# Half of each key and value load added onto the other half by the DMA

## The chip, the cores and the metric

One Trainium2 core runs the kernel. It has TensorE (PE; PEld is its weight load), VectorE (DVE), ScalarE (ACT), GpSimd (POOL) and SyncE (SP), each with its own instruction queue that is worked off in order, and 16 DMA engines that all queues share. The metric is the device time of one execution in microseconds (us). A profiled execution comes beside the timed ones; times "from the span's start" are read from its trace.

## The reference

Attention with pooled keys and values, then a feed-forward layer with a maximum of three products. All inputs and the output are f32.

```python
# q, k, v: (8, 8, 576, 64) = batch, heads, rows, head width
k_p = k.reshape(B, H, 72, 8, D).mean(axis=3)        # mean of each eight rows
v_p = v.reshape(B, H, 72, 8, D).mean(axis=3)
scores = scale * np.matmul(q, k_p.transpose(0, 1, 3, 2))
attn = softmax(scores)
attn_out = np.matmul(attn, v_p)
x = attn_out.transpose(0, 2, 1, 3).reshape(B * S, H * D)      # 4608 x 512
h = np.maximum(np.maximum(x @ w1, x @ w2), x @ w3)            # 512 -> 768
out = h @ w_out                                                # 768 -> 512
```

The change touches the two means: eight rows of keys, or of values, are added up for each of 8 x 72 groups in each of the 8 batches. (The kernel forms sums; the factor 1/8 is put in elsewhere.)

## The kernel before

**Stages.** Attention runs by batch (576 rows each), the feed-forward by block of 512 rows (9 blocks). The work of a batch is laid between the products of the block before, so that TensorE always has something: block n carries the attention of batch n + 1. The order is written out by hand. `block(0, ...)` is the first stage; the dictionary `MIDDLE` holds one string for each of the blocks 1 to 5, which `middle(n)` plays; `ORDER` holds the rest. In `MIDDLE` a step `h` is a product of the feed-forward (`-` begins it, `+` puts its end), a digit is an output product, `a`, `b`, `f` and `S` are VectorE sums, `k` turns folded keys for the scores, `s` are scores, `v` the product with the values, `x` the transpose of its result, `T` the transposed load of queries. A stage between 53 and 160 us takes some 21.5 us.

**Loads.** From batch 1 on, `load_k`, `load_v` and `load_q` (L73 to L101) each bring 576 KB (written) of one batch from memory by a GpSimd DMA, which reads f32 and writes f16 or bf16: 1.18 MB are read. Each kind of tile has two buffers, so batch b + 2 goes where batch b was. A step such as `k5<` in `MIDDLE` issues the load of keys of batch 5.

**Folds.** `fold_steps` (L157) adds the eight rows in three adds: four rows to four rows into `half` (L163, in two parts in the middle stages), two to two (L165), one to one into `kp` (keys) or `vp` (values) (L167). GpSimd does it from batch 2 on for keys and for values of batch 1 and later. `k5+2` plays two of the four instructions of the keys of batch 5.

**What ties GpSimd.** `pool_step` (L879) plays these steps. A load is tied to the last feed-forward product so far, `mms[-1]`, and to the last transposed load of queries, `turned`:

```python
op = load()
for x in (mms[-1], *turned):
    after([op], x)
return
```

After a `!` the next fold instruction is tied to the last VectorE sum (`held[:] = gate`). GpSimd waits for what an instruction needs and all behind it in its queue waits too.

**What uses the folds.** `keys` (L200) transposes `kp` on TensorE (the pkt matmuls of L202), `turn_k` copies the result to `kz` (L213), the scores use that (L226). `values` (L298) multiplies with `vp` (L302). The queries come through `load_q`, and from batch 3 on through a DMA transpose from SyncE's queue (L349), which waits for the queries' landing.

Of the kernel before, what the change touches and what calls it, by code (L numbers as in the profile page):

```python
# [10 lines left out]
ALU = mybir.AluOpType  # L11
# [3 lines left out]
def kernel(  # L15
# [11 lines left out]
    nc = tc.nc  # L27
# [39 lines left out]
    def after(loads, first):  # L67
        for x in loads:
            tc.add_manual_dep(x.ins, first.ins.name, mybir.DependencyInfo(
                mybir.DependencyClass.Sync, mybir.DependencyReason.DATA),  # L70
                reason="weights first")

# [81 lines left out]
    def fold(e, t, out, dtype=F32):  # L154
        return list(fold_steps(e, t, out, dtype))

# [713 lines left out]
    load_k(3, nc.gpsimd)  # L870
    load_v(3, nc.gpsimd)
    load_q(3)
    fold_k(2, nc.gpsimd)
    fold_v(2)
# [4 lines left out]
    def pool_step(n, name):  # L879

        what, b = name[0], int(name[1])
        if name[2:] == "<":
            load = {"k": lambda: load_k(b, nc.gpsimd), "v": lambda: load_v(b, nc.gpsimd),
                    "q": lambda: load_q(b)}[what]
            op = load()
            for x in (mms[-1], *turned):
                after([op], x)
            return
        if (what, b) not in folding:
            if what == "k":  # L890
                new_kp(b)
                folding[what, b] = fold_steps(nc.gpsimd, kts[b], kps[b], parts=2)
            else:
                folding[what, b] = fold_steps(nc.gpsimd, vts[b], vp_all[:, b, :, 0:D],
                                                  parts=2)
        for _ in range(int(name[3:])):
            op = next(folding[what, b])
            for x in held:
                after([op], x)
            held.clear()  # L900
# [14 lines left out]
    def weave():  # L915

        products, seen, outs = {}, {}, out_seven(5)
        for name in ORDER.split():
            if name == "F":
                next(tiles)  # L920
            elif name == "vpool":
                held[:] = gate
                pool_step(5, "v7+4")
# [25 lines left out]
    MIDDLE = {  # L949
        1: """  # L950
            h- q4< k4< h+ 1:x2 1:v4- h- h- v4< h+ 1:v4+ h+ h- 1:x3 h- h+ h+ h- 1:x4 h+ h- k-
            h- h+ h+ q0 h h- k+ h+ h q1 h s0- s0+ s0+ q2 h- s0+ h- s0+ h+ b1 S q3 h+ h- S S
            3:T S h+ a3 s3- a1 s3+ s3+ h- s3+ h- h+ h+ a2 h- s3+ a4 s6- s6+ 1- s6+ h+ b3 b2
            b4 v0 2- 1+ 6- x0 v1 7- v2- 6+ x1 5- 2+ 7+ v2+ ! k3+4 v3- v3+2 v3+ 5+ v4 3- x2
            4- x3 3+ 4+ x4
        """,
        2: """
            h k5< k- h- k+ h+ a1 a3 h- a2 f a4 f ! v3+2 v5< h+ f s0- s0+ s0+ s0+ h- h- h- h+
            h+ s0+ h- h+ s3- h+ h- f s3+ h- s3+ h+ h- s3+ b1 s3+ s6- h+ s6+ h- h+ h- s6+ !
            k4+2 h+ h+ b2 b3 b4 ! k4+2 1- 4:T v0- 1+ v1- v0+ x0 2- v1+ 6- v2- 7- x1 2+ 7+  # L960
            v4+2 6+ v2+ 5- v3- 5+ v3+ x2 x3 v4 x4 3- 4 3+
        """,
        3: """
            k- q5< k+ a3 k6< h a1 h- h- h+ a2 s0- f a4 ! v4+2 s0+ s0+ f h- h+ s0+ h+ s0+ h-
            h- h+ h+ s3- h- v6< h+ h s3+ s3+ s3+ s3+ h- b1 h- h+ h+ s6- s6+ ! k5+2 h h- s6+
            1- h+ b2 b3 b4 1+ ! k5+2 v5+2 v0- 2- v0+ x0 v1 6- 2+ x1 6+ 7- 5:T 7+ v2- 5- v2+
            x2 v3- 5+ v3+ v4 x3 3 x4 4
        """,
        4: """
            h- q6< h+ k- h- k+ a1 a2 f h+ h- a3 a4 ! v5+2 h- f h+ k7< h+ s0- s0+ h- h- s0+  # L970
            s0+ h+ s0+ h+ 6:T h- s3- h+ s3+ s3+ s3+ h- s3+ h+ h- b1 h+ h ! k6+2 s6- s6+ h h
            b3 b2 b4 s6+ ! k6+2 1- v6+2 v0 2- 1+ x0 v1- 6- v1+ 2+ x1 v2 7- 6+ 5- x2 v3 6:k-
            x3 7+ 5+ 3- 6:k+ v4 x4 4- 3+ 4+
        """,
        5: """
            h q7< a1 v7< h- a2 h- a3 h+ h+ a4 ! v6+2 h- s0- s0+ h+ s0+ h- s0+ s0+ h- h- k7+4
            h+ h+ s3- h+ 7:T s3+ h- s3+ h- s3+ s3+ h+ s6- h+ s6+ s6+ h h- v0 h+ h- x0 v1- h+
            v1+ x1
        """}
    folds = iter([f for wi in range(1, 3) for f in [fold_w(wi)] * 4])  # L980

    def middle(n):

        pieces, outs, out_tiles = hidden(n), None, project(n)
        for name in MIDDLE[n].split():
            if name[0] == "h":
                parts(name, lambda: next(pieces))
            elif name == "F":
                next(out_tiles)
            elif name == "f":  # L990
                next(next(folds))
            elif name == "!":
                held[:] = gate
            elif name[0].isdigit() and name[1:] in ("", "+", "-"):
                outs = outs or out_seven(n)
                parts(f"o{name}", lambda: outs(int(name[0]), 0, 1))
            elif name[0] in "ab":
                sums_of(n, name)
            elif name[2:3] == "<" or name[2:3] == "+" and name[3:]:
                pool_step(n, name)  # L1000
            else:
                b, _, step = name.rpartition(":")
                do(int(b or n + 1), step)
        assert next(pieces, None) is None

    tt_all.append(const.tile([128, 4, 5, HALF], F16, name="tt", tag="tt"))
    for n in range(1, 6):
        middle(n)
# [50 lines left out]
```

## Time and profile before

| what | value |
|---|---|
| median of the runs | 227.42 us (227.27 to 227.57, 2 runs) |
| profiled execution: time / span | 227.08 / 225.4 us |
| granted TensorE clock | 1.00 |
| busy: TensorE / VectorE / ScalarE / GpSimd | 212.3 / 161.4 / 120.3 / 140.9 us |
| DMA queue of GpSimd (q0) | 16944 packets, 16.98 MB, 47.8% of 16 engines |
| DMA queue of SyncE (q1) | 29888 packets, 15.87 MB, 31.1% |
| GpSimd's first adds (L163) of values / keys in halves | 10 of 2.12 us / 10 of 1.64 us |
| second adds (L165) of values / keys | 7 of 2.47 us / 6 of 1.81 us |
| last adds (L167) of values / keys | 7 of 1.36 us / 6 of 0.99 us |

Busy times are instruction times put end to end without double counting; an engine that is not the bottleneck loses nothing by idling. A wait is idle time on an engine, with the engine or the DMA that ended it. A DMA's landing is counted from the start of its issue. A DMA share of 1 means that packets were under way on all 16 engines; as several queues can be under way at once it can be above 1 in a short stretch.

### The profile page before, as it was taken

What the parts mean: (1) busy time and instruction counts of PE and PEld (TensorE: products, weight loads), DVE (VectorE), ACT (ScalarE), POOL (GpSimd) and SP (SyncE); (2) the same over time, 40 slices, a digit from 0 to 9 for tenths busy, and PEclk for the clock granted to TensorE, in tenths of its full rate; (3) what the DMA queues carried; (4) which work ended last, traced back from release to release, by engine and by line L of the source; (5) the groups of instructions that cost most, each with busy time, mean ns of one, the idle gap of its engine ahead of it and who ended that gap; (6) DMA issues with size and microseconds to landing.
All of it is one profiled execution on the core that took longest, in us unless ns stands there. A gap on an engine that the chain in (4) does not pass through costs nothing.

```text
span 225.4 us, 4876 instructions
## 1 busy us (share of the span) xinstructions
PE 212.3 (94%) x1884; PEld 147.1 (65%) x1885; DVE 161.4 (72%) x314; ACT 120.3 (53%) x233; POOL 140.9 (63%) x121
## 2 busy tenths in 40 slices
PE   6688999999999999999999999999799999999993
PEld 2477744458658645964685468547589667788882
DVE  3668898036997796776679668729767977878940
ACT  2267524855883576237724842693694445564330
POOL 7974300999939969775885769794292903881020
PEclk9999999999999999999999999999999999999999
DMA  6999999999649999649967999699530755200265
GB/s 179 209 197 197 211 203 209 202 168 230 115 105 156 168 176 247 122 61 214 252 85 154 221 202 151 86 236 166 109 56 19 163 102 113 47 0 3 66 198 159
DMA packets 47303, 33.55 MB, mean 149 GB/s; under 512 B 26992, under 2 KB 42288, under 8 KB 47280
## 3 DMA queue, kind: packets, MB, share of 16 engines
q0 software_dynamic: 16944, 16.98, 47.8%
q1 hardware_dynamic: 29888, 15.87, 31.1%
q10 hardware_dynamic: 448, 0.39, 0.7%
q8 instruction: 15, 0.25, 0.5%
q14 instruction: 8, 0.07, 0.1%
HBM read 34.60 MB, written 9.44 MB: 195 GB/s over the span
## 4 chain that ended last, share of the span: by engine, by line
PE 58%; DMA 17%; DVE 10%; POOL 7%; ACT 3%; issue 3%; ACTq 0%; POOLq 0%; DVEq 0%
PE pw L419 17%; PE oA L765 12%; DMA vt<-in_v_dram 8%; PE oC L765 6%; PE pA L842 5%; DMA mw<-in_moe_w_dram 4%; DMA qT<-qb 4%; PE oB L765 3%; PE pC L842 3%; PE pav L302 2%; PE po L471 2%; PE psc L226 2%; POOL half L163 2%; DVE kz L213 2%; DVE tt L664 1%
## 5 line engine op out<-in xcount | busy, mean ns | idle before, releaser
L419 PE MATMUL pw<-xT,mw 128*128 128x512 f16 (+1 forms) x336 | 68.5, 349 | 0.3 <-ACT xT L296 0.2
L419 PEld LDWEIGHTS <-mw 128*128 128x128 f16 x336 | 30.7, 98 | 26.1 <-issue 1.8
L163 POOL TENSOR_TENSOR half<-vt 72x1024 f32<-72x1024 f16 (+1 forms) x12 | 29.1, 2444 | 20.8 <-DMA vt<-in_v_dram 13.3
L427 DVE TENSOR_TENSOR hT<-t,pw 128x512 f16<-128x512 f16 (+1 forms) x42 | 25.3, 608 | 19.1 <-PE pw L419 11.3
L231 ACT ACTIVATE et<-psc 72x512 f16<-72x512 f32 (+2 forms) x66 | 33.9, 571 | 6.7 <-PE psc L226 6.5
L165 POOL TENSOR_TENSOR half<-half 72x1024 f32<-72x1024 f32 (+1 forms) x13 | 28.1, 2165 | 12.6 <-DVE tt L664 5.2
L425 ACT ACTIVATE t<-pw 128x512 f16<-128x512 f32 (+1 forms) x42 | 22.6, 538 | 15.1 <-PE pw L419 14.5
L312 DVE TENSOR_TENSOR xn<-pav,rcp 128x512 f16<-128x512 f32 x40 | 27.6, 691 | 1.4
L776 ACT COPY osb<-oA 128x512 f32<-128x512 f32 x20 | 11.7, 587 | 20.1 <-PE oA L765 19.9
L851 ACT CAST pad<-pA 128x512 f16<-128x512 f32 x27 | 15.1, 585 | 11.7 <-PE pA L842 9.1
L765 PEld LDWEIGHTS <-tt 128*128 128x128 f16 x200 | 18.8, 98 | 2.1
L163 POOL TENSOR_TENSOR half<-ktFalse 96x768 f32<-96x768 f16 (+1 forms) x11 | 19.3, 1773 | 0.6 <-issue 0.5
L226 PEld LDWEIGHTS <-kz 64*128 64x128 bf16 (+1 forms) x161 | 8.9, 95 | 12.4 <-issue 7.2
L302 PEld LDWEIGHTS <-et 72*128 72x128 f16 x320 | 14.9, 98 | 3.0 <-issue 1.1
L302 PE MATMUL pav<-vp,et 72*128 72x65 f16 x320 | 16.3, 194 | 0.6 <-POOL vp L167 0.3
L310 DVE RECIPROCAL rcp<-pav 128x8 f32<-128x8 f32 x40 | 8.1, 201 | 11.3 <-PE pav L302 11.2
L842 PEld LDWEIGHTS <-sw 128*128 128x128 f16 x144 | 13.8, 98 | 2.7 <-issue 0.2
L822 DVE SCALAR_TENSOR_TENSOR hT<-pad 128x512 f16<-128x512 f16 x18 | 14.0, 785 | 1.1 <-ACT pad L855 0.5
L819 DVE TENSOR_TENSOR pad<-pad,pC 128x512 f16<-128x512 f16 x18 | 12.3, 681 | 3.5 <-PE pC L842 2.7
L226 PE MATMUL psc<-qT,kz 64*128 64x256 bf16 (+5 forms) x138 | 13.3, 263 | 1.0 <-DVE qT L197 0.9
L616 POOL TENSOR_TENSOR pad<-xT 128x256 f16<-128x256 f16 x8 | 5.5, 687 | 13.1 <-DMA xT<-xn 13.1
L765 PEld LDWEIGHTS <-hT 128*128 128x128 f16 x126 | 12.3, 98 | 1.4
(122 smaller groups left out, 400.6 us busy)
## 6 DMA issues: line engine op xcount, KB each, us to landing
out_dram<-osb SPq DMA_DIRECT2D x32, 128.0 KB, 4.6
ktFalse<-in_k_dram POOLq DMA_DIRECT2D x7, 576.0 KB, 9.1
qb<-in_q_dram POOLq DMA_DIRECT2D x7, 576.0 KB, 7.6
vt<-in_v_dram POOLq DMA_DIRECT2D x7, 576.0 KB, 11.8
out_dram<-osb SPq DMA_DIRECT2D x11, 256.0 KB, 6.8
mw<-in_moe_w_dram POOLq DMA_DIRECT2D x9, 256.0 KB, 9.2
ktTrue<-in_k_dram SPq DMA_DIRECT2D x3, 384.0 KB, 5.1
out_dram<-ob SPq DMA_DIRECT2D x8, 128.0 KB, 2.9
```

The costliest lines, as they stand in the source:

```text
L163: yield e.tensor_tensor(out=f[:, at], in0=t[:, at, 0:4, :], in1=t[:, at, 4:8, :], op=ALU.add)
L165: yield e.tensor_tensor(out=f[:, :, 0:2, :], in0=f[:, :, 0:2, :], in1=f[:, :, 2:4, :], op=ALU.add)
L226: nc.tensor.matmul(out, kz_all[b % 2][f % 2][rows, h, :], qTs[b][rows, n + i0:n + i1, 64 * (h % 2):64 * (h % 2) + 64], start=True, stop=True)
L231: nc.scalar.activation(out=out, in_=in_, func=FT.Exp, scale=1.0 / 64.0)
L302: nc.tensor.matmul(pav[:, h // 4, 65 * (h % 4):65 * (h % 4) + 65], ets[b][:, h, c0:c0 + 128], vp_all[:, b, h, :], start=True, stop=True)
L312: nc.vector.tensor_tensor(out=xn, in0=pv[:, :, :, 0:D], in1=rcp.to_broadcast([128, 2, 4, D]), op=ALU.mult)
L419: mm = nc.tensor.matmul(pw, w_sb[wi][:, kc, bass.ts(jc, 128)], x[:, kc], start=(kc == 0), stop=(kc == KCH - 1))
L425: yield lambda t=t, pw=pw: nc.scalar.activation(out=t, in_=pw, func=FT.Relu)
L427: yield lambda t=t, pw=pw: nc.vector.tensor_tensor(out=hT[:, jc, c0:c1], in0=t, in1=pw, op=ALU.max)
L765: nc.tensor.matmul(p, left, right, stop=(r == 4), skip_group_check=True, start=(i in FIRST and r == 0 and (m == 0 or n == LAST)))
L842: mm = nc.tensor.matmul(p[:, w], a[:, kc, bass.ts(g, 128)], b[:, kc, :], start=(i in FIRST and w + kc == 0), stop=(w + kc == 2), skip_grou ...
L851: nc.scalar.copy(out=kept(i, g), in_=p)
```

## The change

For batches 3 to 7 a load of keys or values is cut in two. The first half, `load_half(b, what, 0)` (step `k5<`), brings rows 0 to 3 of each eight as f32 into a tile of the same bytes as before (half the rows, twice the width). The second, `load_half(b, what, 1)` (step `k5>`), brings rows 4 to 7 with the DMA's add onto the same tile. GpSimd then does the two remaining adds in place, in f32 (`fold_four`). Both halves are issued by GpSimd; the second must find the first landed. The five strings of `MIDDLE` are joined into one, each step with its block's number ahead; steps of other engines keep their order. Where the strings said `+4` they now say `+2`, and so on.

```diff
+    def load_half(b, what, late):
+        if not late:
+            shape = [96, 6, POOL // 2, D] if what == "k" else [Sp, H, POOL // 2, D]
+            (kts if what == "k" else vts)[b] = ld.tile(
+                shape, F32, name="kf" if what == "k" else "vf",
+                tag="ktFalse" if what == "k" else "vt")
+        t = (kts if what == "k" else vts)[b]
+        src = (k[b].rearrange("h s d -> (h s d)").rearrange(
+            "(p i j d) -> p i j d", p=96, i=6, j=POOL) if what == "k" else
+            v[b].rearrange("h (sp j) d -> sp h j d", j=POOL))
+        return nc.gpsimd.dma_start(out=t, in_=src[:, :, 4 * late:4 * late + 4],
+                                   accum_op=ALU.add if late else ALU.bypass)
...
+    def fold_four(e, f, out):
+        yield e.tensor_tensor(out=f[:, :, 0:2, :], in0=f[:, :, 0:2, :],
+                              in1=f[:, :, 2:4, :], op=ALU.add)
+        yield e.tensor_tensor(out=out, in0=f[:, :, 0, :], in1=f[:, :, 1, :], op=ALU.add)
...
-    load_k(3, nc.gpsimd)
-    load_v(3, nc.gpsimd)
+    load_half(3, "k", 0)
+    load_half(3, "v", 0)
     load_q(3)
     fold_k(2, nc.gpsimd)
+    load_half(3, "k", 1)
+    load_half(3, "v", 1)
     fold_v(2)
...
-        if name[2:] == "<":
-            load = {"k": lambda: load_k(b, nc.gpsimd), "v": lambda: load_v(b, nc.gpsimd),
-                    "q": lambda: load_q(b)}[what]
-            op = load()
+        if name[2:] in ("<", ">"):
+            op = load_q(b) if what == "q" else load_half(b, what, int(name[2] == ">"))
             for x in (mms[-1], *turned):
                 after([op], x)
...
-                folding[what, b] = fold_steps(nc.gpsimd, kts[b], kps[b], parts=2)
+                folding[what, b] = fold_four(nc.gpsimd, kts[b], kps[b])
```

GpSimd's queue before and after, in the order of the program (`a` to `c` are the three adds, an `a` with a 2 is in two parts):

```
before: q4 k4 v4 | k3a2 k3b k3c v3a2 | k5 | v3b v3c | v5 | k4a2 k4b k4c v4a2 | q5 k6 | v4b v4c | v6 |
        k5a2 k5b k5c v5a2 | q6 | v5b v5c | k7 | k6a2 k6b k6c v6a2 | q7 v7 | v6b v6c | k7a2 k7b k7c v7a2 v7b v7c
after:  k3> v3> (v2's fold) q4 k4< v4< k4> | k3b k3c | v4> | v3b | k5< | v3c | k5> v5< | k4b | v5> | k4c v4b |
        q5 k6< | v4c | k6> v6< | k5b | v6> | k5c v5b | q6 | v5c | k7< | k6b | k7> | k6c v6b | q7 v7< | v6c |
        v7> | k7b k7c v7b v7c
```

In the joined string, `k7>` stands behind `6:T`, the transposed load of the queries of batch 6; the load `k7<`, like `k7<` before, stands ahead of it.

## The prediction

> **What bounds the kernel now.** I read the busy times first, then the table by stretches, then TensorE's waits, then GpSimd's order of work in the stretch that the change touches (47 to 157 us).
>
> The page's busy times, then two rows of the table by stretches (stretch, length, busy us of PE, PEld, DVE, ACT, POOL with counts; granted clock, DMA share, GB/s):
>
> ```profile
> PE 212.3 (94%) x1884; PEld 147.1 (65%) x1885; DVE 161.4 (72%) x314; ACT 120.3 (53%) x233; POOL 140.9 (63%) x121
> ```
> ```profile
> 0.00:47.00 47.00, 41.90 (x346) 24.82 (x348) 29.44 (x64) 24.40 (x45) 26.45 (x35) 1.00 1.17 200
> 47.00:157.00 110.00, 108.73 (x972) 70.94 (x972) 81.93 (x163) 62.12 (x124) 86.62 (x57) 1.00 0.91 166
> ```
>
> From 47 to 157 us TensorE idles 110.00 - 108.73 = 1.3 us, at a granted clock of 1.00. Nothing that relieves GpSimd can win more than that there. TensorE's waits from 47 to 181 us (what waited, for whom: us, times, longest):
>
> ```profile
> PE psf L226 <- DMA qT<-qb: 1.6, 1, 1.6
> PE oA L765 <- ACT osb L776: 0.7, 4, 0.3
> PE psf L226 <- ACT et L231: 0.5, 1, 0.5
> PE pC L842 <- DVE pad L819: 0.4, 1, 0.4
> PE pav L302 <- POOL vp L167: 0.3, 1, 0.3
> ```
>
> GpSimd made TensorE wait 0.3 us, once. The largest wait, 1.6 us, is for the transposed queries of batch 7 at 159.8 us. So the best case is about 1.3 + 1.6 = 2.9 us, short of the 2% (4.5 us) that a measurement of this kernel can tell from no change. What matters is whether the folds stay on time. GpSimd in the first stage touched (start, us), and TensorE's first uses of the folded keys (the pkt transposes, batches 3, 4 and 6):
>
> ```profile
> 67.12 0.77 POOL L99 DMA_DIRECT2D qb<-in_q_dram  x1 [3.71 <-PE oA L765]
> 67.88 0.54 POOL L79 DMA_DIRECT2D ktFalse<-in_k_dram  x1
> 68.42 0.85 POOL L91 DMA_DIRECT2D vt<-in_v_dram  x1
> 69.29 3.24 POOL L163 TENSOR_TENSOR half<-ktFalse 96x768 f32<-96x768 f16 x2
> 72.61 1.81 POOL L165 TENSOR_TENSOR half<-half 96x768 f32<-96x768 f32 x1
> 74.50 0.99 POOL L167 TENSOR_TENSOR kp<-half 96x384 bf16<-96x384 f32 x1
> ```
> ```profile
> 77.28 0.29 PE L202 MATMUL pkt<-ident,kp 96*128 96x96 bf16 x3
> ...
> 98.26 0.29 PE L202 MATMUL pkt<-ident,kp 96*128 96x96 bf16 x3
> ...
> 138.54 0.29 PE L202 MATMUL pkt<-ident,kp 96*128 96x96 bf16 x3
> ```
>
> Folded keys of batch 3 are ready at 75.5, and wanted at 77.28: 1.8 us of room. For batches 4 to 6 I read the same pair: ready at 94.7, 116.1, 137.7; wanted at 98.26, 120.72, 138.54. TensorE takes its work in order, so a late fold stops everything behind it.
>
> **What is removed.** Per batch GpSimd loses the first add: two of 1.64 us (keys) and two of 2.12 us (values), 7.5 us, 37.6 us over five batches. The order of instructions on TensorE, VectorE, ScalarE and SyncE is unchanged; only GpSimd's is. By the waits above none of the 37.6 us is on the path.
>
> **What is added.** Two more DMA issues per batch, and five others of another form. A plain half load moves 576 rows of 1 KB like the load of values (576 rows, 0.86 us to issue); keys cost 0.54 in one piece, so keys' issue grows by 0.3. An issue with the add is not in the trace: between 0.86 and twice that, 1.7, since it names the tile as source too; I take 1.2, near the lower. Together some 13 us, less than the 37.6.
>
> **Waits are added**, and they are the point. The add must find the first half landed, so GpSimd itself waits at each such issue, with folds queued behind it. That needs landing times.
>
> Loads of 576 KB (1.18 MB of f32 read) land behind each other at 72.6, 77.1, 80.2 (batch 4: queries, keys, values) and at 52.9, 58.4, 62.4 (batch 3): 3.1 to 5.5 us apart, mean 4.3. In the first 47 us, with a DMA share of 1.17, they come 3.2 us apart, (48.2 - 32.4) / 5. Loads with a clear queue land 6.8, 7.2 and 7.1 us after issue, so 2.7 us are latency. The weights, with 0.52 MB read and 0.26 written, land 1.3 to 1.5 us apart there: bytes read set the pace. So a plain half load (0.59 MB read) takes 2.15 us of queue; by bytes written it would be 4.3, the other end.
>
> The half with the add reads the same from memory and the tile besides: two reads, 4.3 us. Its ends are 2.15 (the tile's read hidden) and 10.2 (the slowest DMA in the middle, a transposed load of queries, which also reads and writes SBUF; these land in 4.0 to 10.2). I take 4.3, nearest to a row of known bytes. [...]
>
> Per batch the queue gets 2 x 2.15 = 4.3 us more in a stage of 21.5 us: a share of 0.91 + 0.20 = 1.11, just under the 1.17 that the first stretch shows.
>
> **The sum**, following GpSimd from 46.85 (a landing is issue + 2.7 + queue time, or the landing ahead + queue time):
>
> - Batch 3: first halves land at 51.7 and 53.9, before GpSimd reaches the adds at 55.4 behind the folded keys of batch 2: no wait. Two issues (2.4) ahead of the fold of batch 2's values, 8.2 us, end it at 66.0; TensorE wants it at 66.91. Queries land at 58.2 instead of 62.4, so the transposed load that held the next loads until 67.1 is done by then.
> - Batch 4: queries, keys, values issued from 66.0. Queries land at 73.0, the half of the keys at 75.2. GpSimd waits there, with the fold of batch 3's keys behind it: 75.2 + 1.2 + 1.81 + 0.08 + 0.99 = 79.3. Wanted at 77.28: **2.0 late**.
> - Block 2: keys of batch 5 issued at 83, behind two adds, land at 88.6; their add and the values' half follow, which land behind that add at 97.8; its add, 1.2, and the last add of batch 4's keys, 1.0: 100.0, wanted at 98.26 + 2.0. **0.3 early.**
> - Block 3, the same with queries ahead: 111.7, then 120.8, keys of batch 5 done at 123.0, wanted at 122.7. **0.3 late.**
> - Block 4: the add of batch 7's keys stands behind the transposed load of batch 6, and a GpSimd load is tied to the last one issued. Before, that load started at 129.87 and landed at 139.9, with no load tied to it that mattered. Now the queries of batch 6 land at 132.5, so with 8 us (half the keys' bytes beside it) it lands at 140.5; then 0.1 + 1.2 + 1.0 put batch 6's last key add at 142.8, wanted at 138.54 + 2.3. **2.0 late.** Bounds, with 4.0 and 10.2 for that load: 0 and 4.2.
> - Batch 7: the values' half lands at 156.4, its add and the keys' fold (1.2 + 2.9) end at 160.5, wanted at 155.72 + 4.3. **0.4 late.**
>
> Values are never wanted sooner than they are ready. Together 4.7 us. On the profiled execution 227.08 + 4.7 = 231.8 us; the runs' median is 0.34 above it, so **232.1 us**, 2.1% slower. If issues with the add cost 0.86 and landings are 0.1 sooner, this chain gives 1.9, so 229.3.
>
> **The rivals.**
>
> 1. *The queue becomes the bound* (on the same side, larger). From an add of about 5.0 us the share passes 1.17: 0.91 + 2 x (5.0 + 2.15 - 4.3) / 21.5 = 1.18. At 6.4 us, one and a half loads, batch 5's half waits behind two longer adds (+4.2) and the values' behind one (+2.1), and block 3 repeats the second at both landings (+4.2): some 10 more, 241 to 242 us. For it: DMA is busy at 0.91 already and transposed loads reach 10.2 us. Against: half of the bytes come from SBUF.
> 2. *The waits are hidden* (no slower). If the add goes at the pace of the plain half and loads land 3.2 us apart as in the first stretch, batch 4's half lands at 72 to 73, the fold of batch 3 ends in time, and only the transposed load of batch 6 can still cost 0 to 1.5: 227.2 to 229. For it: adds of batch 3 show no wait even in my sum. Against: middle landings were never that close but once (3.1).
> 3. *Relief of VectorE* (the other side). One VectorE subtraction took 2.58 us beside a GpSimd fold where its like took 0.41. With half of the folds gone such blocks shrink. In this kernel it decides only if the waits of rival 2 are hidden as well: TensorE's waits for VectorE and ScalarE in these stages, 0.7 + 0.5, and up to 1 us of the 1.6 at 159.8 would go, 225.2 to 226.8. [...]
>
> That the change does not do what it says has little room: the adds left are two of the three, in f32.
>
> **Chances.** Forecast (2 to 7 us late, 229.4 to 234.4) 0.42; rival 1 0.26; rival 2 0.27; rival 3 0.05. Above 232.0 (slower by over 2%) lie rival 1 and over half of the forecast: 0.50. Within 2%: 0.48. Faster by over 2%: 0.02, since 2.9 us is all there is. The forecast's own range is 229.4 to 234.4; the range for 8 in 10 runs from 226.6 (most of rival 3 below it) to 243 (the longest adds above).
>
> **What would show it.** Right: GpSimd idle before the issues of the second halves, ended by DMA landings of 5 to 9 us; waits of TensorE's pkt transposes or of the kz copies at batches 3 and 6; halves landing about 5 us after issue on a clear queue, the adding ones about 7. Wrong: adds landing in under 5 us (rival 2) or over 9 with a DMA share past 1.17 in 75 to 140 us (rival 1). A wait that I do not see on ScalarE or VectorE would also break the sum.

## The result and the profile after

The changed kernel takes **257.34 us** (median of 2 runs, 256.79 to 257.89) against 227.42 us before: a ratio of 1.132, 95% interval 1.121 to 1.143, 29.9 us slower. The prediction, 232.1 us with a range to 243.0, had the sign and a sixth of the size. The profiled execution shown below took 256.79 us, its span 255.1 us (225.4 before).

The page of the changed kernel, busy times and the two DMA queues (packets, MB, time of the packets as a share of 16 engines' span):

```profile
PE 221.6 (87%) x1884; PEld 150.0 (59%) x1885; DVE 171.9 (67%) x314; ACT 120.2 (47%) x233; POOL 117.7 (46%) x111
...
q0 software_dynamic: 21184, 22.89, 53.6%
q1 hardware_dynamic: 29888, 15.87, 32.4%
```

GpSimd did get 23 us less to do (117.7 for 140.9). TensorE is busy 9.3 us longer with the same 1884 instructions (221.6 for 212.3), and idle for the other 20.4 us of the 29.7 that the span grew. Share times span gives the DMA time: GpSimd's queue 136.7 us (107.7 before), SyncE's 82.7 us (70.1), although SyncE moves the same packets and bytes.

The table by stretches of the changed kernel, the stretch that the change touches and the next (length, busy us of PE, PEld, DVE, ACT, POOL; granted clock, DMA share, GB/s):

```profile
47.00:157.00 110.00, 92.83 (x766) 57.68 (x766) 72.85 (x130) 50.36 (x101) 56.20 (x41) 0.92 1.01 177
157.00:190.00 33.00, 26.52 (x220) 17.34 (x219) 22.46 (x40) 12.99 (x26) 11.93 (x9) 0.90 1.05 163
```

Before, TensorE was busy for 108.73 of the first 110 us, at a clock of 1.00 and a DMA share of 0.91. TensorE's waits from 47 to 190 us in the changed kernel (total, times, longest):

```profile
PE pkt L222 <- POOL kp L175: 16.2, 5, 6.8
PE pav L322 <- DVE xn L332: 2.4, 1, 2.4
PE pw L439 <- DVE hT L447: 2.4, 1, 2.4
```

The first line is new: five waits, one for each batch, for the folded keys. The transposes of the folded keys of batches 3 to 7 on TensorE's timeline (start, length; in brackets the wait before them):

```profile
84.34 0.42 PE L222 MATMUL pkt<-ident,kp 96*128 96x96 bf16 x3 [2.65 <-POOL kp L175]
...
110.91 0.30 PE L222 MATMUL pkt<-ident,kp 96*128 96x96 bf16 x3 [0.25 <-POOL kp L175]
...
142.05 0.42 PE L222 MATMUL pkt<-ident,kp 96*128 96x96 bf16 x3 [6.83 <-POOL kp L175]
...
163.76 0.30 PE L222 MATMUL pkt<-ident,kp 96*128 96x96 bf16 x3 [2.06 <-POOL kp L175]
...
185.09 0.42 PE L222 MATMUL pkt<-ident,kp 96*128 96x96 bf16 x3 [4.41 <-POOL kp L175]
```

They stood at 77.28, 98.26, 120.72, 138.54 and 155.72 before: late by 7.1, 12.7, 21.3, 25.2 and 29.4 us. Each batch adds 4 to 9 us, and after the last nothing more is lost. The five waits make 16.2 us of the 29.4, the two for VectorE (`xn`, `hT`) 4.8; most of the rest is a lower clock behind the waits (see "A lower clock" below). GpSimd in the first stage touched:

```profile
65.64 1.33 POOL L187 TENSOR_TENSOR vp<-half 72x512 f16<-72x512 f32 x1
71.08 0.82 POOL L113 DMA_DIRECT2D qb<-in_q_dram  x1 [4.11 <-DMA qT<-qb]
71.89 0.77 POOL L84 DMA_DIRECT2D kf<-in_k_dram  x1
72.65 0.88 POOL L84 DMA_DIRECT2D vf<-in_v_dram  x1
80.16 1.23 POOL L84 DMA_DIRECT2D kf<-in_k_dram  x1 [6.63 <-DMA kf<-in_k_dram]
80.94 2.28 POOL L173 TENSOR_TENSOR kf<-kf 96x768 f32<-96x768 f32 x1
83.30 0.99 POOL L175 TENSOR_TENSOR kp<-kf 96x384 bf16<-96x384 f32 x1
```

Two waits are seen. GpSimd waits 6.63 us for the first half of the keys of batch 4, with the fold of batch 3's keys behind it: that one was predicted. Before it, GpSimd waits 4.11 us for the transposed queries of batch 3: that one was not. The transposed load was issued at 60.71 and took 9.8 us (view of the DMA issues; before 4.0), beside the two adding halves of batch 3, which landed at 63.4 and 68.6.

The wait for `hT` comes before both. It starts with a VectorE subtraction at 59.70, under GpSimd's first add of the values of batch 2 (one line each from the timelines of GpSimd, VectorE and TensorE):

```profile
58.32 4.62 POOL L183 TENSOR_TENSOR half<-vt 72x2048 f32<-72x2048 f16 x1
59.70 3.67 DVE L684 TENSOR_TENSOR tt<-hT 128x768 f16<-128x768 f16 x1
66.50 3.16 PE L439 MATMUL pw<-xT,mw 128*128 128x512 f16 x8 [2.44 <-DVE hT L447]
```

Before, GpSimd's add ran from 55.17 to 59.23, and the same subtraction, at 59.21, took 0.56 us. Now the two adding issues stand ahead of GpSimd's add and push it onto the subtraction, which ends 0.4 us after it. TensorE waits 2.44 us for the sum behind it, does the next eight products at half clock (0.50 from 66.95 us; 3.16 us, where the eight at 59.63 took 1.89), and is 4.4 us late before it first waits for folded keys (84.34 less the wait of 2.65, for 77.28); 0.5 of that is older. The delay shrinks with the overlap: in e3_late and e7_keys below, where one issue stands ahead of that add, the subtraction takes 1.6 us, in e2_nochain, with two plain issues, 2.0; each time it ends 0.4 us after GpSimd's add.

### The profile page after: what moved, and what is told of

It is laid out like the page before. It is cut to its first block, busy times and chain, and to the rows that moved or that the text cites. A ratio compares the mean times of both kernels' runs of the same rounds, so it can differ in the third digit from the quotient of the medians.

```text
span 255.1 us, 4869 instructions
## 1 busy us (share of the span) xinstructions
PE 221.6 (87%) x1884; PEld 150.0 (59%) x1885; DVE 171.9 (67%) x314; ACT 120.2 (47%) x233; POOL 117.7 (46%) x111
## 4 chain that ended last, share of the span: by engine, by line
PE 34%; DMA 12%; POOL 6%; issue 4%; DVE 3%; ACT 1%; POOLq 0%; DVEq 0%
PE pw L439 9%; PE oA L785 6%; PE pA L862 5%; DMA kf<-in_k_dram 5%; DMA vf<-in_v_dram 5%; PE oC L785 3%; PE pC L862 2%; DMA qT<-qb 2%; PE po L491 2%; POOL kp L175 2%; POOL vf L84 2%; POOL kf L173 1%; PE oB L785 1%; PE psc L246 1%; PE pav L322 1%
## 5 line engine op out<-in xcount | busy, mean ns | idle before, releaser
L439 PE MATMUL pw<-xT,mw 128*128 128x512 f16 (+1 forms) x336 | 73.1, 364 | 4.3 <-DVE hT L447 2.4
L439 PEld LDWEIGHTS <-mw 128*128 128x128 f16 x336 | 31.6, 101 | 33.1 <-issue 11.2
L447 DVE TENSOR_TENSOR hT<-t,pw 128x512 f16<-128x512 f16 (+1 forms) x42 | 25.3, 607 | 21.3 <-PE pw L439 12.5
L84 POOL DMA_DIRECT2D kf<-in_k_dram x10 | 10.8, 1084 | 29.8 <-PE oA L785 17.2
L84 POOL DMA_DIRECT2D vf<-in_v_dram x10 | 12.3, 1229 | 25.2 <-PE oA L785 9.7
L871 ACT CAST pad<-pA 128x512 f16<-128x512 f32 x27 | 15.1, 585 | 16.8 <-PE pA L862 14.2
L785 PEld LDWEIGHTS <-tt 128*128 128x128 f16 x200 | 20.0, 104 | 3.1
L233 DVE COPY kz<-pkt 64x288 bf16<-64x288 bf16 x18 | 8.7, 481 | 14.2 <-PE pkt L222 13.8
L173 POOL TENSOR_TENSOR vf<-vf 72x1024 f32<-72x1024 f32 x5 | 13.8, 2761 | 6.0 <-DVE pad L636 6.0
L222 PE MATMUL pkt<-ident,kp 96*128 96x96 bf16 x21 | 2.5, 236 | 16.2 <-POOL kp L175 16.2
L862 PEld LDWEIGHTS <-sw 128*128 128x128 f16 x144 | 13.9, 98 | 2.6 <-issue 0.2
L183 POOL TENSOR_TENSOR half<-vt 72x2048 f32<-72x2048 f16 x2 | 8.7, 4338 | 13.6 <-DMA vt<-in_v_dram 13.6
L785 PE MATMUL oA<-so,tt 128*128 128x256 f16 x100 | 14.7, 302 | 0.0
## 6 DMA issues: line engine op xcount, KB each, us to landing
ktFalse<-in_k_dram POOLq DMA_DIRECT2D x2, 576.0 KB, 18.5
```

Of the source, the lines that this page charges most:

```text
L84: return nc.gpsimd.dma_start(out=t, in_=src[:, :, 4 * late:4 * late + 4], accum_op=ALU.add if late else ALU.bypass)
L173: yield e.tensor_tensor(out=f[:, :, 0:2, :], in0=f[:, :, 0:2, :], in1=f[:, :, 2:4, :], op=ALU.add)
L439: mm = nc.tensor.matmul(pw, w_sb[wi][:, kc, bass.ts(jc, 128)], x[:, kc], start=(kc == 0), stop=(kc == KCH - 1))
L447: yield lambda t=t, pw=pw: nc.vector.tensor_tensor(out=hT[:, jc, c0:c1], in0=t, in1=pw, op=ALU.max)
L785: nc.tensor.matmul(p, left, right, stop=(r == 4), skip_group_check=True, start=(i in FIRST and r == 0 and (m == 0 or n == LAST)))
L862: mm = nc.tensor.matmul(p[:, w], a[:, kc, bass.ts(g, 128)], b[:, kc, :], start=(i in FIRST and w + kc == 0), stop=(w + kc == 2), skip_grou ...
```

## The experiments

Two theories at first. **Place of the waits**: GpSimd waits at each adding half, with folds behind it, and two round trips through its queue (first half lands, the add is issued, it lands) stretch a batch. **DMA time**: the adding halves fill the queues, whoever waits where. Each kernel ran once, beside a run of the kernel before (226.86 to 227.88 us), so no interval can be given for these times. The last two columns are queue share times span.

| kernel | edit to the changed kernel | us | GpSimd's queue, us | SyncE's queue, us |
|---|---|---|---|---|
| (before) | | 227.42 | 107.7 | 70.1 |
| (changed) | none | 257.34 | 136.7 | 82.7 |
| e1_plain | second halves without the add | 239.88 | 113.9 | 82.4 |
| e2_nochain | plain halves, no wait between them, f16 | 236.09 | 121.1 | 81.8 |
| e3_late | adding halves issued later | 255.14 | 135.8 | 87.4 |
| e6_spread | the same, behind all folds that are due sooner | 263.15 | 142.7 | 92.5 |
| e7_keys | values whole as before | 244.27 | 124.6 | 78.1 |
| e8_noq | no plain query loads of batches 4 to 7 | 238.88 | 121.2 | 79.0 |
| e9_noturn | no transposed query loads of batches 4 to 7 | 252.97 | 138.2 | 63.1 |
| e11_f16 | halves in f16 tiles | 248.04 | 131.7 | 77.8 |
| e12_spareadd | adds onto a spare tile, no chain | 264.52 | 139.5 | 108.2 |
| e13_spareplain | the same, loaded plainly | 245.55 | 119.2 | 88.7 |

### The add or the chain: e1_plain, e2_nochain

```diff
@@ e1_plain @@
-                                   accum_op=ALU.add if late else ALU.bypass)
+                                   accum_op=ALU.bypass)
@@ e2_nochain @@
-            shape = [96, 6, POOL // 2, D] if what == "k" else [Sp, H, POOL // 2, D]
+            shape = [96, 6, POOL, D] if what == "k" else [Sp, H, POOL, D]
-                shape, F32, name="kf" if what == "k" else "vf",
+                shape, F16, name="kf" if what == "k" else "vf",
-        return nc.gpsimd.dma_start(out=t, in_=src[:, :, 4 * late:4 * late + 4],
-                                   accum_op=ALU.add if late else ALU.bypass)
+        return nc.gpsimd.dma_start(out=t[:, :, 4 * late:4 * late + 4],
+                                   in_=src[:, :, 4 * late:4 * late + 4])
```

> The changed kernel, but the second half is loaded plainly onto the first (no add); the sums then hold rows 4 to 7 alone. Same issues, same waits, same folds. Theory A (the time goes to the waits that GpSimd makes for first halves, with folds queued behind them): most of the loss stays, about 245 to 252 us, since only the second halves land faster. Theory B (the DMA's add is what costs, through a full DMA queue): most of the loss goes, below 235 us.

> The changed kernel, but each tile is again f16 with eight rows: both halves are plain loads into different rows, so the second waits for nothing; GpSimd folds rows 0 to 3 alone (rows 4 to 7 are left out of the sums). Same number of issues and the same shorter folds. Theory A: 226 to 231 us. Theory B says the same here. A third theory, that twice as many issues on GpSimd or the shorter folds' places cost the time, expects over 240 us.

Measured: 239.88 and 236.09 us. In e1_plain every issue, wait and fold is kept, and only the addition in the DMA is gone: **17.5 us of the 29.9 go with it**. Second halves land in a mean of 6.6 us, against 8.8 with the add. What is left, 12.5 us, is there without any add; TensorE waits for folded keys (4.0 us), for a transposed `xT` (3.3) and for VectorE's `hT` (2.2). SyncE's queue takes 82.4 us in this kernel too, so its growth comes with the halves and not with the add. e2_nochain has no chain and no add, writes half the bytes, and is still 9 us above the kernel before; its longest waits of TensorE are for SyncE's transposes, 2.5 us for `xT` and 2.3 for `qT`. Both times lie between what the theories had said. Its transposed load of batch 4 took 15.1 us (83.5 to 98.6) beside three halves.

### Moving the waits: e3_late, e6_spread

```diff
@@ e3_late @@
-        v4< k4> 1/h+
+        v4< 1/h+
...
-        ! k3+2 v4> 2:v3- v3+1 2:v3+
+        ! k3+2 k4> 2:v3- v3+1 v4> 2:v3+
...
-        ! v3+1 k5> v5< 2/h+
+        ! v3+1 v5< 2/h+
...
-        ! k4+1 v5> 2/h+
+        ! k4+1 k5> 2/h+
...
-        v4+1 2/6+
+        v4+1 v5> 2/6+
...
@@ e6_spread @@
-        ! k3+2 v4> 2:v3- v3+1 2:v3+
+        ! k3+2 2:v3- v3+1 k4> v4> 2:v3+
...
-        v4+1 2/6+
+        v4+1 k5> v5> 2/6+
...
```

> The changed kernel with every second half issued later in GpSimd's queue: behind the folds that stood behind it (k4> behind k3's folds, v4> behind v3's second add, k5> behind k4's second add, and so on; v3> behind the fold of batch 2's values). First halves have landed by then, the adds still have most of a stage to land. Theory A: 228 to 234 us. Theory B: above 245 us, since the bytes and adds are the same.

> The changed kernel with each pair of second halves (k4> v4>, k5> v5>, k6> v6>) issued behind all folds of the batch before that are due sooner, k7> behind v6's second add, v7> behind k7's folds. Unlike in e3 no fold of keys has a wait for a first half ahead of it that is newly issued in the same stage. Theory A (position of the waits): 232 to 240 us. Theory B (DMA time: the queue of GpSimd was busy 136.7 us of 16 engines in the changed kernel, 113.9 without the add, 107.7 before): 245 us or more, with waits of TensorE for other things than folded keys.

Measured: 255.14 and 263.15 us. In e6_spread no transpose of folded keys waits any more, and the time is the worse for it. The loss has only moved; TensorE's waits in e6_spread:

```profile
PE pw L439 <- DMA xT<-xn: 18.4, 3, 11.8
PE psf L246 <- DMA qT<-qb: 4.2, 1, 4.2
```

Both tiles come through SyncE's transposed loads. The transposed load of batch 4 took 26.9 us in e6_spread (20.8 in e3_late, 10.2 before). In e3_late one of the new places is itself to blame: the issue of the keys of batch 5 stood ahead of batch 4's last add, and GpSimd waited 13.9 us there. So the place of the waits, in the two orders tried, does not make the loss; it decides who waits.

### A price in a quiet stretch: e4_quiet

The kernel before, with two loads put into a stretch near its end where no other load is under way.

```diff
+                zk = const.tile([96, 6, 4, D], F32, name="zk", tag="half")
+                for a, op in ((0, ALU.bypass), (4, ALU.add)):
+                    nc.gpsimd.dma_start(out=zk, in_=sk[:, :, a:a + 4], accum_op=op)
```

> The kernel before, with two more DMAs near the end, where DMA is idle: a plain half load of keys into a spare f32 tile and the other half added onto it, behind GpSimd's last subtraction at about 200 us; nothing reads them. The landing of each by itself. If the add reads two sources for the one, the plain half lands 4.5 to 5.5 us after issue and the adding one 6 to 7.5. If the add is far slower per byte, 9 us or more. Time as before, 227 to 228 us.

Measured: a plain half lands 5.8 us after its issue, an adding one 6.8, and the issues take 0.76 and 1.20 us. The landing of a lone one is only 1.0 us later. But its packets took 4.1 us of the 16 engines, against 1.8 for the plain one (GpSimd's queue from 211.8 to 218.7 us, 59.7%, and from 205.7 to 211.6, 30.2%; some stores ran beside the adding one): the price on the DMA engines is there in a quiet stretch too, and the landing of a lone transfer hardly shows it. The kernel itself took 229.78 us, over the 227 to 228 expected; an estimated 1.7 us of that come before the added loads, from a stretch at half clock (160.3 to 163.7 us, TensorE busy throughout) behind a wait of 1.8 us for transposed queries.

### How much of it scales: e7_keys, e8_noq, e11_f16

```diff
@@ e7_keys @@
+        if what == "v":
+            return None if late else load_v(b, nc.gpsimd)
@@ e8_noq @@
+            if what == "q":
+                qbs[b] = qbs[3]
+                return
@@ e11_f16 @@
-                shape, F32, name="kf" if what == "k" else "vf",
+                shape, F16, name="kf" if what == "k" else "vf",
```

> The changed kernel with only the keys in halves; values of batches 3 to 7 are loaded whole as f16 and folded in three adds as before, at the places of the first halves. Theory B: about half of the loss, 238 to 244 us. Theory A: GpSimd waits once per stage instead of twice, and the landings of k> no longer stand ahead of v<: 230 to 236 us.

> The changed kernel without the loads of queries of batches 4 to 7 (the transposes read batch 3's tile again, so batches 4 to 7 use wrong queries): four plain loads of 3.7 us of DMA time each are gone, 15 us, about half of what the change added (29 us). Theory B: 240 to 246 us. Theory A: little change, 250 us or more, as the waits for first halves of keys and values stay; a few us for halves that no longer stand behind queries.

> The changed kernel with the halves' tiles in f16 instead of f32: the same two loads from memory, issues, waits and folds, but half the bytes written, and half the bytes read back by the add. If the add's price goes by bytes (memory 0.59 MB and tile 0.59 MB so far, tile 0.30 MB now), it falls from about 2.3 to 1.2 us of DMA time for each of ten halves, and the time to 242 to 249 us. If it goes by rows or by the addition itself, whatever the type, 253 to 259.

Measured: 244.27, 238.88 and 248.04 us. Half of the adds cost about half (16.9 of 29.9 us over the kernel before). Leaving out 15 us of ordinary loads from GpSimd's queue gives back 18.5 us with every add in place, a little more than expected (240 to 246 us). Halves in f16 give back 9.3 us, as the bytes would have it, though the DMA time of GpSimd's queue fell by 5.0 us in all, 0.5 for each plain and adding half together, not by 1.1. Over these runs time follows the DMA time of GpSimd's queue: 114 to 125 us of it go with 236 to 246 us, 132 to 143 with 248 to 265.

### The clock: e5_heat

```diff
+        for _ in range(40 if b > 2 else 0):
+            nc.tensor.transpose(pkt[:, 0, :], warm[0:96, 0:128], ident[0:96, 0:96])
```

> The changed kernel with 40 dummy transposes on TensorE ahead of each group of pkt transposes from batch 3 on (into the same PSUM tile, overwritten by the real ones), about 3 to 5 us of work where TensorE waits for the folded keys. If the lower granted clock after a wait (0.57 to 0.82 in four-us windows behind the waits of batches 3 to 7) comes from TensorE standing idle, part of the 9.3 us by which TensorE's busy time grew comes back: 250 to 254 us, clock nearer to 1. If the clock has another cause (DMA, total load), the time is 257 or more.

Measured: 268.24 us, granted clock 0.955. The added work moved the loads into another meeting (the transposed load of batch 4 took 25.7 us, one wait for folded keys 17.4), so this says nothing on the clock. The traces further down do.

### The transposed load: e9_noturn, e10_tail, e14_tail2

The long transposed loads made a third theory: a transposed load beside adding halves holds everything up.

```diff
@@ e9_noturn @@
+            elif name[0] == "T" and b > 3:
+                qTs[b] = qTs[3]
@@ e10_tail, e14_tail2: behind the last matmul of the kernel before @@
+            new.append(nc.gpsimd.dma_start(out=zs[i], in_=src[:, :, 0:4], accum_op=...))
+            nc.sync.dma_start_transpose(out=zT[i], in_=zq.rearrange("p hp t d -> p (hp t d)"))
```

> The changed kernel without the transposed loads of the queries of batches 4 to 7 (their scores read batch 3's transposed tile; the plain loads of the queries still run). In the changed kernel the one of batch 3 took 9.8 us and in runs where more halves stood beside it 20 to 27 us. If DMA time alone counts, four loads of about 4 us less give what leaving out 15 us of plain query loads gave, 237 to 242 us. If a transposed load beside adding halves is what makes the loss large (it holds up all that is under way), the time falls further, to 228 to 235, and adding halves land in 6 to 8 us instead of a mean of 8.8. If neither counts and the adds are slow by themselves, it stays at 248 or more.

> The kernel before, and after its last matmul, with nothing else left but output, five steps in a row, each begun when the one ahead has landed: three plain half loads of keys; one transposed load of a tile of the queries' size alone; the same transposed load with three plain half loads; two adding halves and a plain one; the transposed load with two adding halves and a plain one. The time itself says nothing, the landings do. If DMA time adds up: three plain ones 8 to 10 us, the transposed one alone 4 to 5, with three plain ones 9 to 12, two adds and a plain one 10 to 13, with the transposed one 13 to 16. If a transposed load and adding halves disturb each other beyond their sum, the last step takes 18 us or more and the transposed load lands last or nearly last in it; if the number of 1-KB rows disturbs it already, the third step takes over 14.

e9_noturn: 252.97 us, only 4.4 us less. So the transposed load of queries is not what makes the loss large. Without it TensorE's waits are nearly all for folded keys (15.9 us), and GpSimd's own queue is seen as the bound. Its timeline there:

```profile
106.66 1.39 POOL L84 DMA_DIRECT2D vf<-in_v_dram  x1 [6.23 <-DVE osb L801]
...
110.80 1.33 POOL L113 DMA_DIRECT2D qb<-in_q_dram  x1
111.60 1.22 POOL L84 DMA_DIRECT2D kf<-in_k_dram  x1
...
127.26 1.23 POOL L84 DMA_DIRECT2D kf<-in_k_dram  x1 [11.67 <-DMA kf<-in_k_dram]
```

An add of values, a load of queries and a first half of keys are issued within 6 us and land behind each other at 117.2, 124.7 and 126.7; only then can the add of the keys be issued, and the last add of batch 5's keys stands behind that issue.

e10_tail missed its aim: the transposed load had moved its bytes (2.0 us at 260 to 290 GB/s) before the first half's packets came, so the two hardly met. Even so, in the step with three plain halves it landed 8.9 us after its issue, not 3.9: from 233.5 to 236.2 us 2304 of its 2336 packets went, and the last 32 only by 241, among those of the halves. It did give prices: 2.22 us of DMA time for a plain half, 3.9 for an adding one. e14_tail2 starts the transposed load when the first of five halves has landed.

> The kernel before, and after its last matmul seven steps in a row, each begun when the one ahead has landed: five plain half loads of keys; a transposed load of the queries' size alone; five plain halves again; five plain halves and the transposed load, which now starts only when the first half has landed, so that it meets the others under way; five adding halves; five adding halves and the transposed load in the same way; five adding halves and two transposed loads. Only landings and packet times count. If a transposed load meets nothing worse than its share, it lands 4 to 7 us after its issue each time and its packets take 18 ns as they do alone. If packets of both queues hold each other up on the DMA engines, which is how I now read the middle of the changed kernel (18 to 20 ns for a packet of a transposed load with GpSimd's queue empty, 65 to 115 beside it), the transposed load takes 8 to 12 us beside plain halves and 12 to 20 beside adding ones, at 50 ns and more for each packet, and the step lasts longer than the sum of its parts.

Step by step the DMA queues of e14_tail2. Five plain halves alone (15.45 us long), then five adding halves alone (23.49 us):

```profile
q0 software_dynamic: 800, 2.95, 76.2%
```

```profile
q0 software_dynamic: 2960, 2.95, 90.7%
```

So 0.762 x 15.45 / 5 = **2.35 us for a plain half, and 0.907 x 23.49 / 5 = 4.26 us for an adding one**. The transposed load alone (a stretch of 4.4 us), beside five plain halves (17.97 us), beside five adding halves (28.4 us); the last number of the zT lines is its landing:

```profile
q1 hardware_dynamic: 2336, 0.59, 59.2%
...
zT<-zq SPq DMA_TRANSPOSE x1, 3.9
```

```profile
q1 hardware_dynamic: 2336, 0.59, 25.4%
...
zT<-zq SPq DMA_TRANSPOSE x1, 12.4
```

```profile
q1 hardware_dynamic: 2336, 0.59, 29.2%
...
zT<-zq SPq DMA_TRANSPOSE x1, 21.3
```

In the mean over its packets (share x length x 16 / packets) these are 18, 31 and 57 ns, and the landing goes from 3.9 to 12.4 and 21.3 us. The steps themselves grow by less than I expected: 17.97 us where the sum of the parts is 15.45 + 3.9 = 19.4, and 28.4 where it is 27.4. So the meeting costs hardly any throughput. What it takes is the transposed load's turn: it lands last, after all that GpSimd had queued ahead of it. The third theory stands only in that form. (A last step, five adding halves and two transposed loads, is like the one before: the first transposed load took 22.0 us.)

The same is in the middle of the kernels: the two DMA queues from 62 to 66 us, first in the kernel before, then in the changed one, each under a transposed load of queries:

```profile
q1 hardware_dynamic: 2325, 0.59, 64.9%
```

```profile
q0 software_dynamic: 572, 0.51, 87.3%
q1 hardware_dynamic: 269, 0.07, 29.0%
```

Before, GpSimd's queue was empty and the transposed load passed 2325 packets at 18 ns. After, it passed 269, at 69 ns. In the trace of e14_tail2 the two queues' packets go side by side only in part of the step. From 312 to 314 us there are 292 packets of the transposed load and 289 of the halves. But the transposed load was issued at 300.24, and up to 306.6 the trace has no packet of it, beside 864 of the halves; from 306.6 to 312 there are 248 beside 584. Alone its first packet came 1.2 us after the issue. Nor are its packets slow only beside those of the halves: from 318 to 320 us there are 489 at 81 ns, beside 27 of the halves. So it is shown that the transposed load lands last, and not what holds it until then.

### Without the chain: e12_spareadd, e13_spareplain

```diff
-        t = (kts if what == "k" else vts)[b]
+        t = spare[what] if late and b > 3 else (kts if what == "k" else vts)[b]
...
+    nc.gpsimd.memset(spare["k"], 0.0)
+    nc.gpsimd.memset(spare["v"], 0.0)
@@ e13_spareplain, besides @@
-                                   accum_op=ALU.add if late else ALU.bypass)
+                                   accum_op=ALU.add if late and b == 3 else ALU.bypass)
```

> The changed kernel with the adding halves of batches 4 to 7 (keys and values) put onto a spare tile that GpSimd cleared before, instead of onto the first half: the same transfers, issues and adds in the DMA, but no adding half waits for its first half, only for the adding half of the batch before. The sums of batches 4 to 7 then hold rows 0 to 3 alone. If the adds' DMA time makes the loss, whatever waits for what, 250 to 259 us. If it is the round trips (first half lands, only then is the add issued, and the next first half lands behind it), the loss falls to that of the two plain halves without a chain, 234 to 241 us. Between, 241 to 250, both count.

> The same with the halves of batches 4 to 7 onto the spare tile loaded plainly, without the add (those of batch 3 add onto their first half as in the changed kernel): neither a chain nor an add's DMA time. With two plain halves and the chain the time was 239.9. If the chain is what costs in that one, 230 to 236 here; if it is twice the loads as such, 237 to 241. The difference to the kernel with adds onto the spare tile is the price of the adds without round trips: by DMA time 15 us or more, by round trips 5 or less.

Measured: 264.52 and 245.55 us. With e1_plain and the changed kernel this makes a table of two by two:

| | with the add | plain | the add costs |
|---|---|---|---|
| second half waits for the first | 257.34 | 239.88 | 17.5 |
| it does not wait | 264.52 | 245.55 | 19.0 |

**The add costs 17 to 19 us in either layout, and no cost of the chain is seen.** The kernels with the chain are even 6 to 7 us faster, by the waits below because it keeps loads out of the way of SyncE's. (The two kernels without it keep the chain and the adds of batch 3, so the plain one still holds two adds. Both took longer than expected, 250 to 259 and 230 to 241 us. Clearing the spare tiles adds nothing to the difference: GpSimd does it while it waits for batch 3's transposed queries, and issues the next load at 71.2, as in the changed kernel.) TensorE's waits in e12_spareadd show where it goes without them:

```profile
PE pw L441 <- DMA xT<-xn: 26.5, 2, 24.9
```

e13_spareplain has one such wait of 11.0 us, and there the table by stretches shows the clock as well (columns as above):

```profile
98.00:102.00 4.00, 3.85 (x48) 3.42 (x46) 2.45 (x7) 0.95 (x2) 1.20 (x1) 1.00 1.28 73
102.00:106.00 4.00, 0.82 (x10) 0.61 (x7) 2.24 (x4) 1.17 (x3) 0.00 (x0) 1.00 1.80 156
106.00:110.00 4.00, 0.00 (x0) 0.00 (x0) 0.00 (x0) 0.00 (x0) 0.00 (x0) 0.71 0.91 138
110.00:114.00 4.00, 0.15 (x1) 0.13 (x2) 0.16 (x1) 0.00 (x0) 1.18 (x2) 0.50 1.33 170
114.00:118.00 4.00, 4.00 (x11) 1.34 (x10) 1.07 (x3) 0.60 (x1) 0.37 (x1) 0.51 1.03 133
118.00:122.00 4.00, 4.00 (x29) 1.78 (x27) 2.63 (x7) 2.75 (x6) 2.15 (x2) 1.00 1.07 331
```

While TensorE idles in these rows the granted clock falls to 0.71 and 0.50, and the first 4 us of work after the wait still run at 0.51. The low clock follows the wait here; it does not cause it. In the changed kernel the clock also fell behind waits of 2.44 and 2.65 us, far shorter than the 11.0 here (next section).

## Why the prediction was wrong

**What bounds the kernel, and what is removed: right.** GpSimd's 37.6 us of adds were not on the path, and nothing came back for them.

**The prices of the issues and of the halves: right.** An issue with the add takes 1.2 to 1.4 us (1.2 said). A plain half takes 2.2 to 2.35 us of queue (2.15), an adding one 3.9 to 4.26 (4.3), measured behind the last matmul; the lone plain half of e4_quiet took 1.8. Where the first halves of batch 4 land behind each other (79.6 and 81.9 in the changed kernel) the distance is 2.3. In DMA time an adding half takes 4.26 / 2.35 = 1.81 times a plain one (e14_tail2); the landing of a lone add grew by 17% only (6.8 for 5.8 us, e4_quiet).

**The first step that failed is in batch 3: "so the transposed load that held the next loads until 67.1 is done by then".** It started 2 us sooner (60.71 for 62.57) and ended 3.9 us later (70.5 for 66.6). The sum had put the adding halves of batch 3 at no cost, since TensorE had room for the fold of batch 2. It did not ask what else was on the DMA engines while they moved. The queries of batch 4 were issued at 71.08 instead of 66.0, all landings of batch 4 moved by 4 to 5 us (the first half of the keys at 79.6, not 75.2), and TensorE's first transposes came 7.1 us late, not 2.0. A smaller miss stands ahead of it: the first half of the values landed at 57.1, not 53.9, so that GpSimd did wait for it, 0.6 us, and ended the fold of batch 2 at 67.0 instead of 66.0. And the sum took TensorE to be on time: by the VectorE subtraction shown above it was 4.4 us late at this point, whatever the keys did. The two added issues were weighed by when they end the fold, not by what the fold then stands beside.

**The same omission runs through the rest of the sum.** "A landing is issue + 2.7 + queue time" counted GpSimd's queue alone. The folded keys of batches 3 to 7 were put at 79.3, 100.0, 123.0, 142.8 and 160.5; TensorE got them at 84.3, 110.9, 142.1, 163.8 and 185.1, each about 5 to 8 us further off than the last in the first three. In block 2 the first half of the keys landed 9.9 us after its issue, not 5.6, with an add of 11.4 us ahead of it and seven stores of SyncE beside it. In block 3, 13.5 us. SyncE's transposes waited in turn, and `mms[-1]` and `turned` tie GpSimd's next loads to what waits for these.

**The share was put at 1.11, "just under the 1.17", and a bound was read from that.** Added up over the load, GpSimd's queue grew by 29.0 us (21.5 by the sum) and SyncE's by 12.6 (none by the sum, and its packets and bytes are unchanged). That is 41.6 us of DMA time, and it does not fit: the 1.17 came from the first stretch, where SyncE's queue made 0.12 of it. From 47 to 157 us the changed kernel reaches 1.01, and SyncE's queue makes 0.36 of that with 14702 packets, 43 ns each in the mean; before it made 0.38 there with 20251, 33 ns each. In e1_plain, without the add, SyncE's queue takes nearly as long (82.4 us); what the add itself put on the engines is the 22.8 us by which GpSimd's queue differs there (136.7 and 113.9). Rival 1, the queue becomes the bound, is the case that came. It was priced 15 us too low (241 to 242), and its condition was wrong: it asked for an add above 5.0 us, and 4.26, as measured, was enough.

**Block 4's tie to the transposed load, 2.0 us with bounds of 0 and 4.2:** that step lost 3.9 us (25.2 less 21.3), within the bounds.

**A lower clock** was not in the sum. TensorE's busy time grew by 9.3 us, and nearly all of it is the clock. In five stretches of the changed kernel, each at the end of a wait or behind it, the granted clock is 0.50: from 66.95, 84.02 and 104.50 for 3.41 us each, from 138.63 and 183.00 for 6.83 each. The table by stretches has the first of them and the sum of all five:

```profile
66.95:70.36 3.41, 3.41 (x13) 1.10 (x12) 3.38 (x9) 1.05 (x3) 0.02 (x1) 0.50 1.07 142
sum 23.89, PE 18.07 PEld 9.87 DVE 14.31 ACT 4.72 POOL 10.82; mean PE 3.61 PEld 1.97 DVE 2.86 ACT 0.94 POOL 2.16
```

TensorE is busy for 18.1 us in them. At the full clock that work would take about half (ten products `oA<-so,tt` took 2.34 us at 105.30, in the third of them, and 1.26 at 161.91 in the kernel before), so an estimate from this row is 9.0 us lost. The first three stretches follow waits of 2.44, 2.65 and 2.4 us (`hT`, the keys of batch 3, `xn`), the others those of 6.83 and 4.41 us; behind the wait of 2.06 us at 163.8 the clock stayed at 1.00. By the same estimate each of these five waits cost 1.5 to 2.4 us more than its own length.

**Rival 3, relief of VectorE,** did not come: VectorE is busy 10.5 us longer (171.9 for 161.4). The subtraction at 59.70 shows why: moved folds met other VectorE work. There is another in VectorE's timeline in the changed kernel, beside a GpSimd issue at 98.63 and a fold from 99.52 to 101.76:

```profile
98.14 0.56 DVE L684 TENSOR_TENSOR tt<-hT,tt 128x768 f16<-128x768 f16 x1
98.62 3.57 DVE L684 TENSOR_TENSOR tt<-hT 128x768 f16<-128x768 f16 x1
```

The second took 3.57 us where its like takes 0.54 to 0.56, and TensorE waited 2.4 us for `xn` behind it. Whether the issue or the fold held this one, the row does not tell. Beside the one at 59.70 GpSimd had only its add under way (58.32 to 62.94): the issue ahead of it had ended at 58.85.

**Left open.** Of the 12.5 us that even the plain halves cost (e1_plain) TensorE's busy time makes 5.5 (217.8 for 212.3), and in three stretches at half clock it is busy for 10.2 us, which explains 5.1 of them by the same estimate; the rest is idle time. The runs do not say how much of that idle time is GpSimd's 6 us of DMA time, how much SyncE's 12 us and how much the moved folds. No run removed SyncE's stores or the transposes of `xn`, so their part in the 12 us is argued from the packets only. No run kept GpSimd's fold of batch 2 at its old place, so what the late subtraction adds to the whole time is open as well. Of the kernels run none is faster than the one before, and by the waits none could have won more than 2.9 us.

## What to carry to other kernels

An add moved from an idle engine into the DMA was paid on the DMA engines here: price it in their time (4.26 us for an adding half, 1.8 times the 2.35 of a plain one), and add it to the queues' load in the stretch where it runs, not to the engine that it relieves. When a transfer grows or splits, look at what the *other* queues have under way: here a transposed load landed behind everything that was queued ahead of it, 21.3 us after its issue instead of 3.9 (e14_tail2). When a fold or an issue moves in a queue, look at what the fold then runs beside: one VectorE operation went from 0.56 to 3.67 us. If moving waits moves the loss without shrinking it, the waits are not the cause: take the work away and see.

## What the runs showed of the hardware that I had not expected

- An adding half travels in other packets: 592 for 576 KB, where a plain half f32 to f32 takes 160 (e14_tail2, 2960 and 800 for five).
- Behind an adding issue GpSimd's records overlap. The add of two rows to two of keys at 80.94 is shown with 2.28 us (1.81 before), but the issue ahead of it ends at 81.39: from there to its end are 1.83 us. It is the issue that is longer (1.23 for 0.77 us), not the add.
- SyncE's queue took 82.7 us for the packets and bytes that took 70.1 before, 82.4 in e1_plain without any add, and 108.2 in e12_spareadd.
- The granted clock fell to 0.50 for 3.4 us behind waits of TensorE of 2.4 to 2.65 us, in e4_quiet behind one of 1.82, and not behind one of 2.06: the length of the wait alone does not tell.
- A DMA share well above 1 can go with little moved: 1.80 with 156 GB/s, and 1.28 with 73, in e13_spareplain.
